# An attention and two-layer expert kernel: the second routing phase spread through the first expert, the first expert's rows ahead of its weights, list columns on VectorE

## Chip, cores and metric

The kernel runs on one core of one Trainium2 chip. The metric is the device time of one execution in microseconds (us), lower is better; runs of a kernel are compared by their median. Engines are named TensorE (PE in the rows, PEld its weight loads), VectorE (DVE), ScalarE (ACT), GpSimd (POOL) and SyncE (SP, which issues DMAs).

## What is computed

Three stages, each fed by the one before. Only the second matters here.

```python
def reference(...):
    attn_out = _attn_ref(q, k, v)             # 4 x 8 heads, 576 positions, 64 wide
    x = attn_out.transpose(0, 2, 1, 3).reshape(2304, 512)
    x = _moe_ref(x, w_gate, w1, w2)           # 8 experts, 1024 wide
    return _moe2_ref(x, w_in, w_out)          # one dense layer, 2048 wide

def _moe_ref(x, w_gate, w1, w2):
    cap = N // E                              # 288 rows for each of 8 experts
    order = np.argsort(-(x @ w_gate).flatten())
    for idx in order:                         # greedy: the highest logit first
        tok, e = idx // E, idx % E
        if assigned[tok] >= 0 or counts[e] >= cap:
            continue
        assigned[tok] = e
        counts[e] += 1
    for e in range(E):
        mask = assigned == e
        out[mask] = np.maximum(x[mask] @ w1[e], 0.0) @ w2[e]
```

## The kernel before

**Stages.** Attention (to about 147 us of the span) writes 2304 rows of 512 numbers to DRAM (`x_dram`) and leaves the gate logits `L` in SBUF. Then come eight routing phases and eight experts E0 to E7 (to about 440 us), then the dense layer in groups A to D, in which TensorE never stops.

**A routing phase** (`Router.phase`, L402) finds which expert fills up next and the list of its 288 rows. It is a chain of small steps: five digit levels, each a VectorE compare (`cmp`, L384), 18 counting matmuls (`cnt`, L467), `fl` on VectorE (L473), one matmul `j8` (L476), `jb` and the next level's `E` on VectorE (L479, L482). A tail follows: `sel`, prefix matmuls `pp` (L512, L513), `ON` (L517) with its matmul `cn` (L546) and reduction `ct` (L548), the columns `R` made on GpSimd by four operations (L536 to L539), a last compare against 96 slots, and 18 matmuls `it` (L551, the list matmul here) that turn one-hot rows into the list. `idx` (L554) is the list as integers, `ii` (L563, through the matmul `ip`) the same list laid out for the output, `exi` (L568) the expert's number. All of `it`, `cnt`, `j8`, `pp`, `cn`, `ip` share one PSUM buffer (tag `rt`). In phase 0 the method `busy` (L387) adds fill matmuls (`idle`) behind the chain's matmuls; `busy(k, 20, im)` puts 20 behind the list matmul.

**Gather and expert.** `gather` (L712) issues three indirect DMAs on GpSimd (`xrow`, 96 rows each) and writes `ilist` from SP. `expert` (L723) reads `exi` into a register on SP, transposes the three row blocks on TensorE (`xtp`, L737), copies them (`xh`, L741), and then for j = 0 to 7 loads a block of 128 hidden units' weights (256 KB of w1, 256 KB of w2), multiplies (`hp`), applies relu (`gh`, `gl`) and, two blocks later, multiplies by w2 into `ya`. E0 and E2 are plain (`MODES`, 'w'): w1 is used as float32 as it was loaded (four `hp` matmuls, shown as eight, x8), and only w2 is split into two parts, a cast on ScalarE (`wbh`, L693) and a subtraction on VectorE (`wbl`, L694). The other six ('s') split w1 too (12 `hp` matmuls). Plain experts load w1 and w2 as two DMAs into buffers of the pools `wa` (4 buffers a tag); the others load one 512 KB block `wraw` into a pool of 8.

**Order.** `ORDER` (L869) lists the steps; a tile scheduler fixes from it one order of instructions per engine, and each engine runs its own in order. A phase is a generator that yields between its steps. 'R0 R1' runs phases 0 and 1 to their end in the program before E0; then each of the 16 steps of an expert advances the routing by one yield (`bg()`), so that phase 2 runs through E0, phase 3 from E0's end through E1, and so on. A phase has 15 yields.

```python
def routing():
    for k in range(8):
        for _ in r.phase(k):
            yield
        rows[k] = f.gather(k, r.out[k][0], r.out[k][2])
        yield
```

Of the kernel before, what the change touches and what calls it, by code (L numbers as in the profile page):

```python
# [336 lines left out]
class Router:  # L337
    def __init__(self, nc, tc, ctx, a):
# [63 lines left out]
    def phase(self, k):  # L402

        nc, wk, sm, L = self.nc, self.wk, self.sm, self.L
        V, Q = nc.vector, nc.gpsimd
# [138 lines left out]
        if not last:  # L544
            cn = self.psr.tile([128, 144], F32, name="cn", tag="rt")
            self.behind(nc.tensor.matmul(cn, self.one, ON.rearrange("p c e -> p (c e)"), start=True, stop=True))  # L546
            ct = sm.tile([128, 8], F32, name="ct")
            V.tensor_reduce(out=ct, in_=cn.rearrange("p (c e) -> p e c", e=8), op=ALU.add, axis=AX.X)  # L548
        it = self.psr.tile([128, 3], F32, name="it", tag="rt")
# [316 lines left out]

ORDER = ('R0 R1 E0/1 E1 E2/2 E3 E4 E5/1 E6/2 E7/2 N A2 A4 A4 A4 A4 B4 B4 B4 B4 B2 C4 C4 C4 C4 C2 D4 D4 D4 D4 D2').split()  # L869
# [131 lines left out]
```

## Time and profile before

| | us |
|---|---|
| timed runs (3): median, lowest, highest | 846.5, 841.11, 850.13 |
| profiled execution | 840.9 |
| its span, first to last instruction | 839.1 |
| TensorE busy in it | 811.0 |
| VectorE busy | 677.6 |
| ScalarE busy | 501.3 |
| GpSimd busy | 181.8 |

The profile is of one execution. Times in rows are microseconds from the span's start, unless ns stands with them. A matmul's end is modelled: successive ones overlap, so the distance from start to start is what one costs. A granted clock of 1.00 is 2.4 GHz, 0.50 is 1.2 GHz.

### The profile page before, as it was taken

How to read it: one execution, taken by the hardware profiler on the slowest of the kernel's cores; microseconds unless marked ns; L12 is line 12 of the kernel's file. 1: busy time of each engine (PE TensorE's matmuls, PEld its weight loads, DVE VectorE, ACT ScalarE, POOL GpSimd, SP SyncE). 2: the span in 40 equal slices, each digit the busy share in tenths (PEclk: the TensorE clock that was granted, in tenths of full speed). 3: DMA queues.
4: the chain of work that ended last, by engine and by line, in shares of the span. 5: the costliest groups of instructions: out<-in, count | busy, mean ns of one | idle time of the engine just before them, and what ended most of it. 6: DMA issues, size and time to landing. Idle time of an engine off the chain costs nothing.

```text
span 839.1 us, 16995 instructions
## 1 busy us (share of the span) xinstructions
PE 811.0 (97%) x6228; PEld 684.5 (82%) x6228; DVE 677.6 (81%) x1813; ACT 501.3 (60%) x1209; POOL 181.8 (22%) x243
## 2 busy tenths in 40 slices
PE   7999999879899999999999999999999999999997
PEld 4787877458898899999998888888878888888886
DVE  6999986848889989998848888788888878657764
ACT  3887876022433535556647677777767777665552
POOL 5565420102211230400000000002223211312223
PEclk9999999979999999999999999999999999999999
DMA  9977622337267796597325444458697674973512
GB/s 223 197 191 223 197 83 103 101 116 254 84 180 237 264 296 214 166 335 247 107 83 177 129 127 131 140 162 201 144 238 179 172 190 107 252 163 123 128 51 76
DMA packets 67411, 142.41 MB, mean 170 GB/s; under 512 B 8224, under 2 KB 20896, under 8 KB 67328
## 3 DMA queue, kind: packets, MB, share of 16 engines
q1 hardware_dynamic: 27008, 70.54, 27.2%
q0 software_dynamic: 29280, 56.63, 26.0%
q10 hardware_dynamic: 11040, 14.16, 4.9%
q8 instruction: 49, 0.80, 0.4%
q14 instruction: 34, 0.28, 0.1%
HBM read 112.98 MB, written 18.88 MB: 157 GB/s over the span
## 4 chain that ended last, share of the span: by engine, by line
PE 77%; DVE 8%; issue 6%; DMA 4%; ACT 2%; POOL 2%; SPq 0%; POOLq 0%; ACTq 0%; DVEq 0%
PE hm L699 7%; PE hm L701 7%; PE hm L700 7%; PE oa L700 6%; PE oa L701 6%; PE oa L699 6%; PE ya L699 4%; PE hp L779 4%; PE ya L700 4%; PE ya L701 4%; PE hp L699 3%; PE hp L701 3%; PE hp L700 3%; PE cnt L467 2%; PE pvl L223 2%
## 5 line engine op out<-in xcount | busy, mean ns | idle before, releaser
L699 PE MATMUL hm<-Yh,wM_sb 128*128 128x512 f32 (+1 forms) x320 | 118.5, 370 | 1.5 <-DMA Yh<-y_dram 1.5
L701 PE MATMUL hm<-Yh,wM_sb 128*128 128x512 f32 (+1 forms) x320 | 118.7, 371 | 0.0
L700 PE MATMUL hm<-Yl,wM_sb 128*128 128x512 f32 (+1 forms) x320 | 118.5, 370 | 0.0
L699 PE MATMUL oa<-wM_sb,gh 128*128 128x512 f32 x288 | 113.1, 393 | 0.0
L700 PE MATMUL oa<-wM_sb,gh 128*128 128x512 f32 x288 | 113.1, 393 | 0.0
L701 PE MATMUL oa<-wM_sb,gl 128*128 128x512 f32 x288 | 112.9, 392 | 0.0
L855 DVE SCALAR_TENSOR_TENSOR eu<-eu 128x512 f32<-128x512 f32 x72 | 49.7, 690 | 45.1 <-ACT eu L854 44.7
L699 PE MATMUL ya<-gh,wbh 128*128 128x288 f32 x256 | 79.5, 315 | 0.3 <-DVE Yl L760 0.3
L700 PE MATMUL ya<-gl,wbh 128*128 128x288 f32 x256 | 77.0, 302 | 0.0
L861 ACT CAST gh<-eu 128x512 fp32r<-128x512 f32 x72 | 44.4, 616 | 53.6 <-DVE eu L858 53.3
L701 PE MATMUL ya<-gh,wbl 128*128 128x288 f32 x256 | 75.9, 298 | 0.0
L699 PEld LDWEIGHTS hm<-Yh,wM_sb 128*128 128x128 f32 x320 | 60.3, 188 | 13.1 <-DMA Yh<-y_dram 2.1
L862 DVE TENSOR_TENSOR gl<-eu,gh 128x512 fp32r<-128x512 f32 x72 | 49.5, 688 | 24.9 <-ACT gh L861 24.3
L700 PEld LDWEIGHTS hm<-Yl,wM_sb 128*128 128x128 f32 x320 | 60.3, 188 | 11.2
L701 PEld LDWEIGHTS hm<-Yh,wM_sb 128*128 128x128 f32 x320 | 60.2, 188 | 10.7
L850 ACT ACTIVATE eu<-hm 128x512 f32<-128x512 f32 x72 | 42.8, 594 | 41.6 <-PE hm L701 41.5
L699 PEld LDWEIGHTS oa<-wM_sb,gh 128*128 128x128 f32 x288 | 54.0, 188 | 12.7 <-ACT osb L826 0.4
L852 ACT ACTIVATE eu<-eu,one_sb 128x512 f32<-128x512 f32 x72 | 52.1, 723 | 20.5 <-DVE eu L851 19.8
L701 PEld LDWEIGHTS oa<-wM_sb,gl 128*128 128x128 f32 x288 | 54.0, 188 | 12.4
L700 PEld LDWEIGHTS oa<-wM_sb,gh 128*128 128x128 f32 x288 | 54.1, 188 | 11.9
L788 ACT ACTIVATE gh<-hp 128x288 fp32r<-128x288 f32 x64 | 26.1, 408 | 61.7 <-PE hp L701 32.1
L827 POOL DMA_DIRECT2D part<-osb x36 | 33.2, 1018 | 135.9 <-ACT osb L826 126.7
(187 smaller groups left out, 2151.5 us busy)
## 6 DMA issues: line engine op xcount, KB each, us to landing
wraw<-in_wE_dram SPq DMA_DIRECT2D x48, 512.0 KB
n<-in_wM_dram SPq DMA_DIRECT2D x32, 512.0 KB
Yh<-y_dram POOLq DMA_DIRECT2D x16, 1024.0 KB, 8.9
Yl<-y_dram POOLq DMA_DIRECT2D x16, 1024.0 KB
part<-osb POOLq DMA_DIRECT2D x36, 256.0 KB, 4.1
vw<-in_vw_dram SPq DMA_DIRECT2D x16, 315.0 KB
kT<-in_kT_dram SPq DMA_DIRECT2D x16, 291.0 KB
qT<-in_qT_dram SPq DMA_DIRECT2D x16, 288.0 KB
```

Of the source, the lines that this page charges most:

```text
L223: self.nc.tensor.matmul(op[c, u], vw[:, 3 * g + u, c], d['aT'][:, u, c], start=True, stop=True)
L699: mm(out, lh, rh, start=first, stop=False)
L700: mm(out, lh, rl, start=False, stop=False)
L701: return mm(out, ll, rh, start=False, stop=last)
L779: self.r.mm = nc.tensor.matmul(hp, w1[:, 128 * dc:128 * dc + 128], xh[:, dc], start=dc == 0, stop=dc == 3)
L788: self.cast = nc.scalar.activation(out=hh[:, 0:288], in_=hp, func=AF.Relu)
L827: nc.gpsimd.dma_start(p, o, accum_op=ALU.add)
L850: nc.scalar.activation(out=e, in_=hp[:, 0:w], func=AF.Exp)
L852: nc.scalar.activation(out=u, in_=e, func=AF.Square, bias=one)
L855: nc.vector.scalar_tensor_tensor(out=u, in0=u, scalar=1.0, in1=r, op0=ALU.add, op1=ALU.mult)
L861: self.cast = nc.scalar.copy(gh[:, 0:w], e)
L862: self.mark = nc.vector.tensor_tensor(out=gl[:, 0:w], in0=e, in1=gh[:, 0:w].bitcast(F32), op=ALU.subtract)
```

## The change

Three things move, and small ones with them.

*Order.* 'R0 R1' becomes 'R0 H4': phase 0 to its end, then four yields of phase 1; the rest of phase 1 advances with the steps of E0, phase 2 follows from E0's end through E1, and phase 7 ends in E5.

*Rows and weights.* All experts load 512 KB blocks `wraw` from the pool of 8; plain experts use w1 in place. In E0 the loads of j = 2 to 7 depend on the third gather (`g0` is overwritten and ends as the third), and the casts of their w2 on the last copy of the transposed rows. 28 fills instead of 20 stand behind phase 0's list matmul.

*List columns.* `R` gets four columns: 0 index, 1 index x g1, 2 index x g2, 3 zero. Columns 0 and 3 are written once, on GpSimd, into two fixed tiles; one VectorE operation writes the other two. After the list matmul two VectorE operations (add 1152, subtract the next column) and a copy to integers give the list. `ON` moves ahead of the prefix matmuls, its matmul joins their PSUM tile, and `ct` is read before the last compare.

```diff
@@ Router.load
+        for t in self.Rw:
+            nc.gpsimd.memset(t[:, :, 3], 0.0)
+            nc.gpsimd.tensor_copy(t[:, :, 0], self.index)
@@ Router.phase
         V.tensor_tensor_scan(out=run[:, 0:n], data0=self.one[:, 0:n], data1=s2, initial=0.0, op0=ALU.mult, op1=ALU.add)
+        if not last:
+            ON = wk.tile([128, 18, 8], F16, name="ON")
+            V.tensor_tensor(out=ON, in0=OH, in1=bc8(ge[:, 0]), op=ALU.mult)
         yield
...
-        pp = self.psr.tile([128, 36], F32, name="pp", tag="rt")
+        pc = self.psr.tile([128, 180], F32, name="pp", tag="rt")
+        pp, cn = pc[:, 0:36], pc[:, 36:180]
+        if not last:
+            self.behind(nc.tensor.matmul(cn, self.one, ON.rearrange("p c e -> p (c e)"), start=True, stop=True))
...
-        if not last:
-            ON = wk.tile([128, 18, 8], F16, name="ON")
-            V.tensor_tensor(out=ON, in0=OH, in1=bc8(ge[:, 0]), op=ALU.mult)
...
-        R = sm.tile([128, 18, 3], F16, name="R")
-        s12 = sm.tile([128, 18], F32, name="s12")
-        Q.tensor_tensor(out=s12, in0=self.index, in1=g1, op=ALU.mult)
-        Q.tensor_tensor(out=R[:, :, 0], in0=self.index, in1=s12, op=ALU.subtract)
-        Q.tensor_tensor(out=R[:, :, 2], in0=self.index, in1=g2, op=ALU.mult)
-        Q.tensor_tensor(out=R[:, :, 1], in0=s12, in1=R[:, :, 2], op=ALU.subtract)
+        R = self.Rw[k % 2]
+        V.tensor_tensor(out=R[:, :, 1:3], in0=g12, in1=two(self.index), op=ALU.mult)
         oa = self.compare(a16, 96, ALU.is_equal, PARTS[k == 0])
+        if not last:
+            ct = sm.tile([128, 8], F32, name="ct")
+            V.tensor_reduce(out=ct, in_=cn.rearrange("p (c e) -> p e c", e=8), op=ALU.add, axis=AX.X)
         yield
...
-        self.busy(k, 20, im)
-        idx = self.pk.tile([96, 3], I32, name="idx")
-        V.tensor_scalar_add(idx, it[0:96], 1152.0)
-        ig = self.igw[k % 2]
-        V.tensor_scalar_add(ig[:, 0:3], it[0:96], 1152.0)
+        self.busy(k, 28, im)
+        ig = self.igw[k % 2]
+        li = ig[:, 0:3]
+        V.tensor_scalar_add(li, it[0:96, 0:3], 1152.0)
+        V.tensor_tensor(out=li, in0=li, in1=it[0:96, 1:4], op=ALU.subtract)
+        idx = self.pk.tile([96, 3], I32, name="idx")
+        V.tensor_copy(idx, li)
@@ FFN.split
-        self.nc.scalar.copy(wh, src)
+        c = self.nc.scalar.copy(wh, src)
+        if self.late is not None:
+            self.tc.add_manual_dep(c.ins, self.late.ins.name, ..., reason="order")
@@ FFN.gather
+            if k == 0:
+                self.g0 = ld
@@ FFN.expert
+            raw = self.rawe.tile([128, 1024], F32, name="wraw")
+            ld = nc.sync.dma_start(raw, src)
+            self.late = xc if k == 0 and j > 1 else None
+            if k == 0 and j > 1:
+                self.tc.add_manual_dep(ld.ins, self.g0.ins.name, ..., reason="rows first")
             if plain:
-                w1 = self.wa.tile([128, 512], F32, name="w1", tag="wah")
-                nc.sync.dma_start(w1, src[:, 0:512])
...
-                    raw = self.wa.tile([128, 512], F32, name="w2r", tag="wal")
-                    nc.sync.dma_start(raw, src[:, 512:1024])
-                    w2 = self.split(raw, self.wb, "wb")
+                w1 = raw[:, 0:512]
+                w2 = self.split(raw[:, 512:1024], self.wb, "wb")
@@ ORDER and body
-ORDER = ('R0 R1 E0/1 E1 E2/2 ...
+ORDER = ('R0 H4 E0/1 E1 E2/2 ...
+            if st[0] == 'H':
+                for _ in range(int(st[1:])):
+                    bg()
+                continue
```

SP at E0's start, before: the register load of the expert's number, then four pairs of loads (w1 `w`, w2 `w2r`, 512 elements a partition each) without any wait for rows, and `ilist` behind them.

```order
L726 TENSOR_LOAD exi [waits DVE_49]
...
L776 DMA w2r<-in_wE_dram 128x512 [waits DMAHW5_49]
L770 DMA w_3686<-in_wE_dram 128x512 [waits DMAHW6_49]
...
L770 DMA w_3798<-in_wE_dram 128x512
L776 DMA w2r<-in_wE_dram 128x512
L720 DMA ilist<-ii 3x96 [waits DMAHW4_49,DVE_49]
```

The same place now: two loads of 1024 elements a partition, and a third that names DMASW2, the semaphore on which the transposes of the third row block wait too.

```order
L776 DMA wraw<-in_wE_dram 128x1024 [waits DMAHW2_49,DMAHW3_49,DMAHW1_49,DMAHW4_49,DMAHW0_49,DMAHW7_49,Activation_49,Pool_49]
L776 DMA wraw<-in_wE_dram 128x1024 [waits DMAHW5_49]
L776 DMA wraw<-in_wE_dram 128x1024 [waits DMAHW6_49,DMASW2_49]
L727 DMA ilist<-ii 3x96 [waits DVE_49]
L776 DMA wraw<-in_wE_dram 128x1024
```

Six of E0's eight loads have moved behind the third gather, and the list's DMA stands behind the first of them.

VectorE in E0's first blocks, before, from the compare of phase 1's second digit level on (`wbl` is the subtraction that splits a block's w2, `gl` the second part of a block's relu; numbers tell tiles apart):

```order
L384 TENSOR_TENSOR cmp_103<-E_3366,rthr_64 128x2304
L458 SCALAR_TENSOR_TENSOR G_3369<-E_3366,dg2_3318 128x18
L473 TENSOR_SCALAR fl_3391<-cnt_3371 128x8
L791 SCALAR_TENSOR_TENSOR gl_3627<-hp_3612,gh_3613 128x288
L479 TENSOR_REDUCE jb_3395<-j8_3393 128x1
L482 TENSOR_SCALAR E_3397<-G_3369,jb_3395 128x36
```

The same place now; wraw_3528 and wraw_3588 are the blocks of j = 2 and j = 3, the first two of the loads that depend on the third gather.

```order
L388 TENSOR_TENSOR cmp_105<-E_3374,rthr_64 128x2304
L462 SCALAR_TENSOR_TENSOR G_3377<-E_3374,dg2_3326 128x18
L699 TENSOR_TENSOR wbl_3531<-wraw_3528,wbh_3530 128x512
L477 TENSOR_SCALAR fl_3399<-cnt_3379 128x8
L699 TENSOR_TENSOR wbl_3591<-wraw_3588,wbh_3590 128x512
L794 SCALAR_TENSOR_TENSOR gl_3445<-hp_3432,gh_3433 128x288
L483 TENSOR_REDUCE jb_3449<-j8_3447 128x1
L486 TENSOR_SCALAR E_3451<-G_3377,jb_3449 128x36
```

Two subtractions have moved between the routing's operations, one ahead of `fl`, one ahead of `jb`; before, the four of the first four blocks stood ahead of this compare.

TensorE in E1 before, from the end of phase 2's list matmul to phase 3's first count:

```order
L551 MATMUL it_4017<-R_3994,cmp_103 128x3
L700 MATMUL hp_4383<-xl_4137,wah_4387 128x288
L701 MATMUL hp_4383<-xh_4136,wal_4388 128x288
...
L561 MATMUL ip_4056<-ident_sb_105,rig0_69 72x96
L701 MATMUL hp_4383<-xh_4136,wal_4388 128x288
L467 MATMUL cnt_4188<-rOH_68,cmp_103 128x8
```

The same place now, with rows of the 12 `hp`, 12 `ya`, 2 `hp` and 9 `ya` matmuls between the two left out:

```order
L552 MATMUL it_4254<-rR0_71,cmp_105 128x4
...
L564 MATMUL ip_4289<-ident_sb_107,rig0_69 72x96
...
L706 MATMUL ya3_4137<-gh_4169,wbl_4177 128x288
L704 MATMUL hp_4411<-xh_3912,wah_4415 128x288
...
L706 MATMUL ya2_4136<-gh_4228,wbl_4236 128x288
L471 MATMUL cnt_4389<-rOH_68,cmp_105 128x8
```

Where five `hp` matmuls and `ip` stood between the list matmul and the count, 35 matmuls and `ip` stand now.

## Rows read from the trace of the kernel before

**Rows 1.** The page, part 1: busy time, share of span, instructions.

```profile
PE 811.0 (97%) x6228; PEld 684.5 (82%) x6228; DVE 677.6 (81%) x1813; ACT 501.3 (60%) x1209; POOL 181.8 (22%) x243
```

**Rows 2.** Stretches: length, then each engine's busy time (instructions), PEclk, DMA share, GB/s.

```profile
core 0: us, PE busy (x) PEld busy (x) DVE busy (x) ACT busy (x) POOL busy (x), PEclk, DMA share, GB/s
...
172.00:176.00 4.00, 2.25 (x28) 1.96 (x29) 0.17 (x1) 1.00 (x2) 0.00 (x0) 0.60 0.15 39
...
180.00:184.00 4.00, 4.00 (x30) 2.83 (x29) 0.70 (x3) 0.41 (x1) 0.00 (x0) 0.62 0.07 9
...
220.00:224.00 4.00, 4.00 (x42) 3.73 (x41) 3.70 (x28) 2.87 (x8) 0.87 (x4) 1.00 0.27 96
224.00:228.00 4.00, 1.87 (x39) 1.66 (x36) 3.59 (x18) 0.93 (x2) 2.62 (x3) 0.93 0.32 101
228.00:232.00 4.00, 4.00 (x23) 3.85 (x22) 3.66 (x10) 0.00 (x0) 1.75 (x2) 0.64 0.65 167
...
348.00:376.00 28.00, 27.57 (x219) 26.69 (x218) 27.07 (x61) 15.97 (x34) 4.43 (x8) 1.00 0.85 287
```

**Rows 3.** TensorE's waits, 150 to 445 us: waiter, releaser, us, times, longest.

```profile
PE it L551 <- DVE ct L548: 1.0, 1, 1.0
PE it L551 <- POOL R L539: 0.6, 1, 0.6
```

**Rows 4.** Timeline of E0's head: start, us, engine, line, instruction, idle before and releaser.

```profile
161.75 0.35 SPq L770 DMA_DIRECT2D w<-in_wE_dram  x1
...
164.85 1.11 POOL L717 DMA_INDIRECT xrow<-x_dram,idx  x1 [2.34 <-DMA w2r<-in_wE_dram]
...
165.39 0.62 ACT L693 CAST wbh<-w2r 128x512 fp32r<-128x512 f32 x1 [18.22 <-DMA w2r<-in_wE_dram]
...
167.63 0.91 POOL L717 DMA_INDIRECT xrow<-x_dram,idx  x1 [0.31 <-issue]
...
173.75 0.90 PE L737 MATMUL xtp<-ident_sb,xrow 96*128 96x96 f32 x4 [4.88 <-DMA xrow<-x_dram,idx]
...
178.40 4.21 PE L779 MATMUL hp<-xh,w 128*128 128x288 f32 x8 [0.57 <-ACT xh L741]
```

**Rows 5.** Timeline of TensorE in E1, at the start of phase 3.

```profile
223.69 0.61 PE L551 MATMUL it<-R,cmp 128*128 128x3 f16 x18
...
227.39 0.63 PE L467 MATMUL cnt<-rOH,cmp 128*128 128x8 f16 x18 [2.13 <-DVE rOH L439]
```

**Rows 6.** Phase 1's list matmul, gathers, E1's transposes; landing of all gathers (last row).

```profile
196.93 0.60 PE L551 MATMUL it<-R,cmp 128*128 128x3 f16 x18
...
198.00 0.92 POOL L717 DMA_INDIRECT xrow<-x_dram,idx  x1 [2.08 <-DVE dg L429]
...
201.55 0.91 POOL L717 DMA_INDIRECT xrow<-x_dram,idx  x1 [0.30 <-issue]
...
212.01 1.15 PE L737 MATMUL xtp<-ident_sb,xrow 96*128 96x96 f32 x12
...
DMA to landing us min/median/max: 5.0/5.3/8.2
```

**Rows 7.** Timeline of one digit level of phase 1 in E0.

```profile
182.40 0.66 PE L467 MATMUL cnt<-rOH,cmp 128*128 128x8 f16 x18
...
183.13 0.17 DVE L473 TENSOR_SCALAR fl<-cnt 128x8 f16<-128x8 f32 x1 [3.92 <-PE cnt L461]
...
183.57 0.17 PE L476 MATMUL j<-fl,rsum 128*128 128x8 f16 x1
...
185.13 0.59 PE L467 MATMUL cnt<-rOH,cmp 128*128 128x8 f16 x18
```

**Rows 8.** Chain that ended last: start, us from piece to piece, what.

```profile
203.53 1.94 PE hp L779 x8
...
361.83 0.27 PE hp L701 x2
...
373.39 0.69 DVE wbl L694
```

**Rows 9.** Timeline: the first compare of a phase.

```profile
225.52 1.34 DVE L384 TENSOR_TENSOR cmp<-E,rthr 128x2304 f16<-128x2304 bf16 x1
```

More of the change, by code (lines that the diff above doesn't have):

```diff
@@ L350, in __init__ @@
         self.igw = [c.tile([96, 72], F32, name=f"rig{i}") for i in range(2)]
+        self.Rw = [c.tile([128, 18, 4], F16, name=f"rR{i}") for i in range(2)]
         for t in self.igw:
@@ L404, in phase @@
         nc, wk, sm, L = self.nc, self.wk, self.sm, self.L
-        V, Q = nc.vector, nc.gpsimd
+        V = nc.vector
         bc8 = lambda t: t.unsqueeze(2).to_broadcast([128, t.shape[1], 8])
@@ L525, in phase @@
             ps = pz[:, 0:18]
-        g1 = sm.tile([128, 18], F32, name="g1")
-        g2 = sm.tile([128, 18], F32, name="g2")
+        g12 = sm.tile([128, 18, 2], F32, name="g12")
+        g1, g2 = g12[:, :, 0], g12[:, :, 1]
         V.tensor_scalar(out=g1, in0=ps, scalar1=97.0, scalar2=None, op0=ALU.is_ge)
@@ L543, in phase @@
             yield
[L544 to L549, printed above, removed]
+        it = self.psr.tile([128, 4], F32, name="it", tag="rt")
         for c in range(18):
             im = self.behind(nc.tensor.matmul(it, oa[c], R[:, c], start=(c == 0), stop=(c == 17)))
-        self.busy(k, 20, im)
+        self.busy(k, 28, im)
[3 more added lines that the diff above has]
+        V.tensor_tensor(out=li, in0=li, in1=it[0:96, 1:4], op=ALU.subtract)
         idx = self.pk.tile([96, 3], I32, name="idx")
-        V.tensor_scalar_add(idx, it[0:96], 1152.0)
-        ig = self.igw[k % 2]
-        V.tensor_scalar_add(ig[:, 0:3], it[0:96], 1152.0)
+        V.tensor_copy(idx, li)
         yield
@@ L684, in __init__ @@
         self.xs = P("f_xs", 1, ctx_e)
-        self.mark = self.cast = None
+        self.mark = self.cast = self.late = None
         self.pend = []
@@ L692, in split @@
         wl = pool.tile([128, 512], F32R, name=nm + "l")
-        self.nc.scalar.copy(wh, src)
+        c = self.nc.scalar.copy(wh, src)
+        if self.late is not None:
+            self.tc.add_manual_dep(c.ins, self.late.ins.name, mybir.DependencyInfo(mybir.DependencyClass.NoSync, mybir.DependencyReason.DATA), reason="order")
         self.nc.vector.tensor_tensor(out=wl, in0=src, in1=wh.bitcast(F32), op=ALU.subtract)
@@ L716, in gather @@
             xr = self.xg.tile([96, 512], F32, name="xrow")
-            nc.gpsimd.indirect_dma_start(out=xr, out_offset=None, in_=self.a['x_dram'],
-                                         in_offset=bass.IndirectOffsetOnAxis(ap=idx[:, g:g + 1], axis=0))
+            ld = nc.gpsimd.indirect_dma_start(out=xr, out_offset=None, in_=self.a['x_dram'],
+                                              in_offset=bass.IndirectOffsetOnAxis(ap=idx[:, g:g + 1], axis=0))
+            if k == 0:
+                self.g0 = ld
             rows.append(xr)
@@ L740, in expert @@
             if plain:
-                (nc.vector.tensor_copy if g == 1 else nc.scalar.copy)(xh[:, :, q], t)
+                xc = (nc.vector.tensor_copy if g == 1 else nc.scalar.copy)(xh[:, :, q], t)
             else:
@@ L767, in expert @@
             hl = None
-            if plain:
-                w1 = self.wa.tile([128, 512], F32, name="w1", tag="wah")
-                nc.sync.dma_start(w1, src[:, 0:512])
-                if mode == 'p':
-                    w2 = self.wb.tile([128, 512], F32, name="w2", tag=("wbh", "wbl")[j % 2])
-                    nc.sync.dma_start(w2, src[:, 512:1024])
-                else:
-                    raw = self.wa.tile([128, 512], F32, name="w2r", tag="wal")
-                    nc.sync.dma_start(raw, src[:, 512:1024])
-                    w2 = self.split(raw, self.wb, "wb")
+            raw = self.rawe.tile([128, 1024], F32, name="wraw")
+            ld = nc.sync.dma_start(raw, src)
+            self.late = xc if k == 0 and j > 1 else None
+            if k == 0 and j > 1:
+                self.tc.add_manual_dep(ld.ins, self.g0.ins.name, mybir.DependencyInfo(mybir.DependencyClass.Sync, mybir.DependencyReason.DATA), reason="rows first")
+            if plain:
+                w1 = raw[:, 0:512]
+                w2 = self.split(raw[:, 512:1024], self.wb, "wb")
                 for dc in range(4):
@@ L780, in expert @@
             else:
-                raw = self.rawe.tile([128, 1024], F32, name="wraw")
-                nc.sync.dma_start(raw, src)
                 w1 = self.split(raw[:, 0:512], self.wa, "wa")
@@ L865, in group @@
             yield
-ORDER = ('R0 R1 E0/1 E1 E2/2 E3 E4 E5/1 E6/2 E7/2 N A2 A4 A4 A4 A4 B4 B4 B4 B4 B2 C4 C4 C4 C4 C2 D4 D4 D4 D4 D2').split()
+ORDER = ('R0 H4 E0/1 E1 E2/2 E3 E4 E5/1 E6/2 E7/2 N A2 A4 A4 A4 A4 B4 B4 B4 B4 B2 C4 C4 C4 C4 C2 D4 D4 D4 D4 D2').split()
 MAN = 0
```

## Prediction

> **What bounds the kernel now.** I read the page first: TensorE is busy for 97% of the span of 839.1 us [rows 1]. The profiled execution took 840.9 us, 1.8 more than its span; the three timed runs have a median of 846.5 (841.11 to 850.13), so my sum is made against 840.9 and scaled to the median at the end. A measurement of this kernel can tell about 1%, some 8.4 us, from no change.
>
> So a gain must come from places where TensorE stands still or runs slowly. The table of stretches finds two of size in the routed experts E0 to E7, 168 to 184 and 224 to 232 [rows 2]; the list of TensorE's waits adds 1.0 us for VectorE's `ct` and 0.6 for GpSimd's `R` [rows 3].
>
> The first place is E0's head [rows 4]. GpSimd issues three gathers from 164.85 to 167.63, the fills run out, and the first transpose starts at 173.75, after 4.9 us of waiting and 8.9 after its gather was issued. Then the granted clock is at its lower level, 0.50 (1.2 of 2.4 GHz), from about 172.9 to 183.0: E0's first eight matmuls take 4.21 us, the same eight elsewhere 1.94 [rows 8]. The second place is the start of routing phase 3 in E1: TensorE has run the list matmul and `ip` and waits 2.13 us, up to 227.39, for `rOH` [rows 5]; after it the clock is low again (0.93 and 0.64 in two stretches of 4 us, so 0.56 + 2.88 = 3.4 us at half speed, 1.7 us lost) [rows 2].
>
> **The change part by part.**
>
> *E0's head.* `ct` stood behind the compare, and the list matmul waited 1.0 us for it [rows 3]; now it stands ahead, and the matmul can end some 0.6 us earlier, near 163.8 (the compare itself ends later than `ct` could). But the list takes three dependent VectorE operations instead of one, with operations of the next phase between them, about 0.8 us more. Net: the gathers start near 165.0, the third at 167.8. Their landing is the unknown. The trace shows three: 5.0, 5.3 and 8.2 us [rows 6]; in E0 it was 8.9 at most, beside eight 256 KB weight loads issued one after the other from 161.75 on [rows 4]. Now two loads of 512 KB go out before the rows, half the bytes, and at E0's pace (the first 512 KB usable at 165.39) most of them are in when the gathers start. I take 5.2: the third block lands at 173.0 (ends: 172.8, and 176.7 with 8.9). Twenty-eight fills of 0.23 us reach from 163.8 to 170.3, where the first block lands, so the eight extra ones (1.8 us) hide in that wait.
>
> From 173.0: third transposes 0.35, copy and hand-over 0.6, so j=0's `hp` starts at 173.95 instead of 178.40. Its four quarters (1.94) and a count block (0.55) end at 176.45 at the full clock; before, this point was the end of the count block of 182.40, 182.95 [rows 7]. Without anything else that is 6.5 us.
>
> But the loads of j=2 to 7 now wait on SP for the third row block. And on VectorE the subtraction that splits j=2's weights has moved ahead of `fl` of the second digit level, while TensorE's `j8` behind j=0 needs that `fl`. Issue at 173.2; from issue to ScalarE's cast 512 KB took 3.64 us (161.75 to 165.39) [rows 4], so 176.9; the cast 0.62 [rows 4], the subtraction 0.69 [rows 8], `fl` to `j8` 0.44 [rows 7]: `j8` at 178.65, a new wait of 2.2 us. j=1 (1.94) and a quarter of j=2 (0.49) follow, to 181.1. The next `jb` stands behind j=3's subtraction, one load later (512 KB are 1.8 us at some 290 GB/s), and a `gl`: 180.4. From `j8` to the count were 1.56 us (183.57 to 185.13) [rows 7], 1.33 of it from `jb`: 181.75, another 0.65 of waiting, and that count is over at 182.25. Before, it was over at 185.6, with a quarter (0.5) less done: gain 185.6 - 182.25 + 0.5 = 3.85. A wait of 2.2 us is as long as the one in E1, after which the low clock cost 1.7; I count half, 0.85. Term: 3.0, between 6.5 (no new wait) and -1.5 (block at 176.7, so 0.15, less 1.7).
>
> A rule of the Trainium skill bears on this (DMA: Bandwidth & Descriptors, Issuing engines are not separate DMA queues): DMAs of all engines run on the same 16 DMA engines and interleave. By it the rows gain from the weights' absence, as 8.9 beside eight weight loads and 5.0 elsewhere suggest. Another rule of that page (Rules for kernel authors, Overlap DMA with compute) speaks against the change: issue early, wait late. By that rule the 2.2 and 0.65 us are the price of holding loads back; no row here shows held loads.
>
> *Start of a phase in E1.* Phase 3 now starts near E1's end, and between the list matmul and the next count TensorE has 12 `hp`, 12 `ya`, 2 `hp` and 9 `ya` matmuls, 35 x 0.135 us = 4.7 [rows 8], with list matmul and `ip` 5.4. VectorE needed 3.7 from there to the count (223.69 to 227.39) [rows 5]; now with a `gl` and two more list operations about 4.5. The wait goes: 2.13 + 1.7 = 3.85 gained; VectorE is next late, by a margin of 0.9. The other starts have as much between. Ends: 0 (the wait turns up in another expert) and 3.85.
>
> *List columns.* The 0.6 us that list matmuls waited for GpSimd go (ends 0 and 0.6). VectorE gets one operation for GpSimd's four, some 0.1 us a phase, beside a TensorE that is the bound; `ON`, the joined PSUM tile, two small copies on GpSimd in the attention part and the plain experts' 512 KB loads hide in the same way, at 0.1 to 0.3 us a phase if that cover goes.
>
> *Later experts.* Half of phase 6 moves from E4 into E5. VectorE is busy 27.1 of 28 us there (348 to 376). The tail of a phase with its list costs it about 3.7 us (220 to 224, 28 operations) [rows 2], two levels with compares of 0.75 some 1.5 more: 32.3 in all. TensorE's share, two counts, list, `pp` and `ip`, is 2.3: 30.3. Up to 2.0 would be lost, unless split weights in buffers and E7's slack take it up. I take -0.7 (ends -2.0 and 0).
>
> *Rows one expert ahead.* For E1, 15.1 us lay between the list matmul (196.93) and the transposes (212.01). Now TensorE has from phase 1's list matmul to E1's first transposes 11 `hp` quarters (5.3 us), 36 `ya` (4.8), two count blocks (1.1) and 0.7 of small ones: 11.9, and 12.7 to the third block's; counted alike 12.0 in E2 and 13.1 or more later. To have the third block takes 2.7 to 2.9 from list matmul to first gather (1.07 before; in E1 a compare of 1.34 [rows 9] now stands before the integer copy), 2.7 to 3.55 from first to third gather (198.00 to 201.55), and 5.0 to 8.2 to land [rows 6]: 10.4 to 14.7. I take -0.5 (ends 0 and, below, -9.25).
>
> Sum: 3.0 + 3.85 + 0.6 - 0.7 - 0.5 = 6.25 us. 840.9 - 6.25 = 834.65, 0.74% less; from the median 846.5 that is **840.2 us**.
>
> **Rivals.**
>
> *No new wait in E0.* The held loads land in time, or don't hold up `fl`. For: the fills keep the clock, and the loads have the DMA engines alone. Against: 3.64 us for 512 KB is what the trace shows. 6.5 + 3.85 + 0.6 - 1.2 = 9.75: 831.2, 1.2% faster.
>
> *The gather is slow by itself.* Its 8.9 us aren't the weights' doing; rows land as late as before and the held loads later still. For: few landings are shown, and one is 8.2. Against: 5.0 and 5.3. -1.5 + 3.85 + 0.6 - 1.2 = 1.75: 839.2, no difference that can be measured.
>
> *Rows late at each expert: slower.* Place: the first transposes of E1 to E3. With 8.9 to land, E1 needs 2.9 + 3.55 + 8.9 = 15.35 against 12.7: 2.65 late; E2, with nothing before its copy, 14.15 against 12.0: 2.15; E3 14.15 against 13.1: 1.05. The first two pull the clock down, 1.7 each: 9.25 lost. It decides from a landing of about 6.5 us on. 3.0 + 3.85 + 0.6 - 0.7 - 9.25 = -2.5: 843.4, slower. Against: two landings of three were short.
>
> **How the numbers follow.** Forecast 0.53, no new wait 0.25, slow gather 0.15, late rows 0.07. Faster by over 1%: most of the second case and the near edge of the first, 0.27. Slower by over 1%: the far edge of late rows with low clock at more experts, 0.05. The rest, 0.68, lies within 1%. The range goes from the second case, scaled 836.7, less the 5.4 by which a run can lie under the median, 831, to late rows, scaled 849.
>
> **What would show it.** Right: E0's third transposes near 173, full clock from 170 to 176; then a wait of about 2 us on TensorE for `fl`, with SP idle until the rows land and VectorE waiting for a cast; no wait for `rOH` in E1; none for GpSimd before list matmuls. Wrong: transposes of E0 later than 175, none of the 2 us, a wait for rows in E1 or E2 over 1 us, or VectorE over 97% in E5 and E6 with TensorE waiting for it.

## Result and profile after

The changed kernel takes 849.92 us (median of 16 runs, 845.2 to 853.92) beside 842.34 us for the kernel before on the same chip (16 runs). By the means it takes 1.0079 times as long, 95% interval 1.0057 to 1.0102. That is 7.6 us slower by the medians and 6.6 by the means, where the prediction had 6.3 faster. The profiled execution took 845.38 us, the second shortest of the 16; its span is 843.6 us, 4.5 more than that of before. TensorE is busy 1.1 us longer than before [rows 1], so again most of the difference lies in standing still, and in the clock:

```profile
PE 812.1 (96%) x6236; PEld 685.1 (81%) x6236; DVE 680.3 (81%) x1829; ACT 501.3 (59%) x1209; POOL 175.2 (21%) x215
```

The table of stretches, with the columns of [rows 2]. The first two rows are E0's head, the next three the end of E3 and the start of E4, the last two lie in E5:

```profile
172.00:176.00 4.00, 3.32 (x38) 2.33 (x36) 2.49 (x6) 0.96 (x2) 0.00 (x0) 1.00 0.44 122
180.00:184.00 4.00, 2.65 (x29) 1.89 (x28) 2.86 (x8) 1.86 (x4) 0.00 (x0) 1.00 0.99 388
308.00:312.00 4.00, 0.00 (x0) 0.00 (x0) 1.09 (x4) 0.48 (x1) 0.00 (x0) 0.82 0.92 227
312.00:316.00 4.00, 3.07 (x17) 2.97 (x18) 1.62 (x4) 1.44 (x3) 0.00 (x0) 0.50 0.02 9
316.00:320.00 4.00, 4.00 (x42) 3.93 (x42) 1.78 (x6) 1.02 (x2) 0.00 (x0) 0.82 0.01 4
...
356.00:360.00 4.00, 2.03 (x8) 1.70 (x8) 4.00 (x12) 0.42 (x1) 0.00 (x0) 0.80 0.80 263
360.00:364.00 4.00, 4.00 (x25) 4.00 (x25) 3.41 (x16) 0.62 (x1) 0.00 (x0) 0.78 0.46 163
```

E0's head runs at the full clock now, where [rows 2] had 0.60 and 0.62. But TensorE does nothing at all for four microseconds at 308, and a new hole is at 356, with VectorE busy for all of the 4.00 us. The list of TensorE's waits from 150 to 445 us gives the names (waiter, releaser, us in total, times, longest):

```profile
PE xtp L744 <- DMA xrow<-x_dram,idx: 6.0, 3, 4.9
PE cnt L471 <- DVE cmp L388: 3.2, 8, 1.3
PE j L480 <- DVE fl L477: 1.8, 2, 1.4
PE hp L704 <- DVE gl L794: 1.4, 1, 1.4
...
PE pp L523 <- DVE run L511: 0.6, 1, 0.6
PE pp L522 <- DVE sel L508: 0.3, 1, 0.3
```

The waits for `ct`, `R` and `rOH` of [rows 3] and [rows 5] are gone. The wait for rows has moved: from E0, where [rows 4] had it, to E4 (4.95 us) and E2 (1.0). E0's head answers to [rows 4] and [rows 7]; this is its timeline on TensorE, VectorE, GpSimd and SP:

```profile
166.48 2.88 POOL L722 DMA_INDIRECT xrow<-x_dram,idx  x1 [42.99 <-DVE wm L437]
...
170.88 0.92 POOL L722 DMA_INDIRECT xrow<-x_dram,idx  x1 [0.31 <-issue]
...
171.63 0.55 PE L744 MATMUL xtp<-ident_sb,xrow 96*128 96x96 f32 x4
...
173.91 0.55 PE L744 MATMUL xtp<-ident_sb,xrow 96*128 96x96 f32 x4
...
174.80 1.39 SPq L776 DMA_DIRECT2D wraw<-in_wE_dram  x3
...
175.03 1.72 PE L784 MATMUL hp<-xh,wraw 128*128 128x288 f32 x6 [0.57 <-ACT xh L748]
...
178.40 0.69 DVE L699 TENSOR_TENSOR wbl<-wraw,wbh 128x512 fp32r<-128x512 f32 x1 [2.63 <-ACT wbh L696]
179.00 0.16 DVE L477 TENSOR_SCALAR fl<-cnt 128x8 f16<-128x8 f32 x1
179.22 0.17 PE L480 MATMUL j<-fl,rsum 128*128 128x8 f16 x1 [1.41 <-DVE fl L477]
...
183.33 0.60 PE L471 MATMUL cnt<-rOH,cmp 128*128 128x8 f16 x18 [1.35 <-DVE cmp L388]
```

The first block lands 5.15 us after its gather (171.63 - 166.48; 8.9 before), and the split of the held block j=2 ends right ahead of `fl`, for which TensorE has stood 1.41 us.

E4's head, on GpSimd and TensorE:

```profile
290.87 0.80 POOL L806 DMA_DIRECT2D Yh<-y_dram  x1 [21.45 <-DMA y_dram<-Yl]
...
292.44 0.78 POOL L806 DMA_DIRECT2D Yl<-y_dram  x1 [0.77 <-DVE na L582]
...
296.05 1.28 POOL L722 DMA_INDIRECT xrow<-x_dram,idx  x1 [2.82 <-PE ip L564]
...
312.93 2.26 PE L744 MATMUL xtp<-ident_sb,xrow 96*128 96x96 f32 x12 [4.95 <-DMA xrow<-x_dram,idx]
```

`Yh` and `Yl` (1 MB each) are the dense layer's input for its second group, issued by GpSimd ahead of time. E4's gathers, issued 3.6 us behind `Yl`, take 16.88 us until the transposes start. The packets of the two DMA queues in use (packets, MB, share of 16 engines; q0 carries what GpSimd issues, q1 the weights that SP issues) in 290.8 to 306.5, and then in 306.5 to 313:

```profile
q1 hardware_dynamic: 936, 3.42, 60.8%
q0 software_dynamic: 1028, 2.10, 42.0%
...
q1 hardware_dynamic: 222, 0.77, 46.4%
q0 software_dynamic: 215, 0.58, 36.4%
```

2.10 MB is `Yh` and `Yl`; 0.58 MB is the rows (3 x 96 x 2 KB = 0.59). So the rows passed after the 2 MB, with E4's weights taking the larger share beside them. Packet by packet the trace has the same order: `Yh` and `Yl` go in 1024 packets of 2 KB, the rows in 144 of 4 KB, and the first of the 144 starts at 305.1, 9.0 us after its gather was issued, when 902 of the 1024 have started.

In the trace of before E4's gathers went out ahead of `Yh` and `Yl`, and 34 us ahead of its transposes:

```profile
281.42 0.92 POOL L717 DMA_INDIRECT xrow<-x_dram,idx  x1 [1.24 <-DVE sg L427]
...
299.76 0.77 POOL L803 DMA_DIRECT2D Yl<-y_dram  x1 [2.06 <-issue]
...
315.64 0.82 PE L737 MATMUL xtp<-ident_sb,xrow 96*128 96x96 f32 x8
```

A delay of 17 us would have cost nothing there.

### The profile page after: what moved, and what is told of

The parts are those of the page before. It is cut to its first block, busy times and chain, and to the rows that moved or that the text cites. A ratio compares the mean times of both kernels' runs of the same rounds, so it can differ in the third digit from the quotient of the medians.

```text
span 843.6 us, 16899 instructions
## 1 busy us (share of the span) xinstructions
PE 812.1 (96%) x6236; PEld 685.1 (81%) x6236; DVE 680.3 (81%) x1829; ACT 501.3 (59%) x1209; POOL 175.2 (21%) x215
## 3 DMA queue, kind: packets, MB, share of 16 engines
q0 software_dynamic: 29280, 56.63, 25.9%
## 4 chain that ended last, share of the span: by engine, by line
PE 58%; issue 6%; DMA 4%; POOL 2%; DVE 1%; ACT 1%; POOLq 0%; DVEq 0%
PE hm L704 7%; PE hm L706 7%; PE hm L705 7%; PE oa L705 6%; PE oa L706 6%; PE oa L704 6%; PE ya L704 3%; DMA xrow<-x_dram,idx 3%; PE ya L706 3%; PE ya L705 3%; PE hp L704 2%; PE hp L705 2%; PE hp L706 2%; PE hp L784 2%; DMA Yh<-y_dram 1%
## 5 line engine op out<-in xcount | busy, mean ns | idle before, releaser
L696 ACT CAST wbh<-wraw 128x512 fp32r<-128x512 f32 x64 | 39.8, 622 | 69.1 <-PE ya L705 40.4
L722 POOL DMA_INDIRECT xrow<-x_dram,idx x24 | 30.7, 1280 | 185.9 <-PE ip L564 95.4
```

Source lines behind the costliest of these rows:

```text
L696: c = self.nc.scalar.copy(wh, src)
L722: ld = nc.gpsimd.indirect_dma_start(out=xr, out_offset=None, in_=self.a['x_dram'], in_offset=bass.IndirectOffsetOnAxis(ap=idx[:, g:g + 1], ...
```

## Experiments

Ratios are to the kernel before, run on the same chip in the same batch, with 95% intervals; they are not quotients of medians. Waits are of one profiled execution each.

### The parts alone

Two runs take one part alone into the kernel before, one takes both, one takes the spread without the list part. The diff of each is the change itself, so much of it.

```diff
 e5_list_only:    Router.load, Router.phase as changed, 20 fills
 e6_rows_only:    FFN.split, FFN.gather, FFN.expert as changed, 28 fills
 e2_order_r1:     both; ORDER = 'R0 R1 E0/1 ...'
 e11_rows_spread: e6_rows_only with ORDER = 'R0 H4 E0/1 ...'
```

> The kernel before with the list columns alone (R on VectorE in fixed tiles, the add, subtract and copy behind the list matmul, ON and its matmul earlier, ct ahead of the last compare); order, loads and 20 fills as before. Theory (this part only takes away the waits for ct, 1.0 us, and for R, 0.6 us): both waits gone, no new one over 0.5 us in E0 to E3, ratio 0.997 to 0.999. Rival (the waits of 1.2 to 1.4 us for fl at the start of phases in E1, E2 and E3, which the changed kernel with the old order has, come from this part): those waits appear here, some 4 us, ratio 1.002 to 1.005.

> The kernel before with the rows and loads alone (512 KB loads for plain experts too, E0's loads of j = 2 to 7 behind the third gather, 28 fills); order and list columns as before. Theory (E0's head gains about 4.5 us in the landing of the rows and the low clock behind it, and gives 1 to 3 back in waits behind the held loads): transposes of E0 end by 175 less whatever the attention part took longer, no low clock there, ratio 0.996 to 0.999. Rival (this part brings the waits in E1 to E3 that the changed kernel with the old order has): ratio 1.002 to 1.005.

> The changed kernel with the order of before: phase 1 to its end ahead of E0 in the program, each phase two experts ahead. Theory (the time was lost by rows one expert ahead, and by VectorE's load in E5): no wait for rows at E2 and E4, none for gl in E5; the wait for rOH at the start of phase 3 in E1 (2.1 us) comes back; E0's head keeps its early rows. Ratio 0.993 to 0.997. Rival (the spread is what gains, and the loss is in the rest of the change): ratio 1.008 or more, the waits in E4 and E5 stay.

> The changed kernel without its list columns: rows and loads as in e6_rows_only, and the new order (second phase spread, each phase one expert ahead). Theory (the spread costs, in late rows, whatever the list columns do): ratio 1.001 to 1.004, with a wait for rows of over 1 us in at least one of E1 to E4. Rival (without the list columns the spread gains, by the start of phase 3 in E1 that no longer waits for rOH): ratio 0.993 to 0.996.

| run | rows first | list part | spread | ratio |
|---|---|---|---|---|
| e6_rows_only | yes | | | 0.9971 (0.9943 to 1.0000) |
| e5_list_only | | yes | | 1.0049 (1.0022 to 1.0076) |
| e2_order_r1 | yes | yes | | 1.0045 (1.0012 to 1.0077) |
| e11_rows_spread | yes | | yes | 1.0070 (1.0027 to 1.0113) |
| the change | yes | yes | yes | 1.0079 (1.0057 to 1.0102) |

Rows first gains 0.3%, as its theory said, with an interval that ends at 1.0000. The spread costs 1.0% beside e6 (with the list part there already, 0.3%, e2 to the change, within their intervals). The 1.0% is a rough size: ten of e11's twelve executions took 843.0 to 858.05 us, the other two 1031.22 and 1559.73. e11 has the same hole as the changed kernel: E4's transposes wait 4.09 us. The list part costs where it was to gain; e5 fits its rival in size, though not in place: its profile has no wait for `fl` in E1 to E3, but 1.2 us for `gl` and 0.5 for `Yl` in E5 (0.2 and 0.3 before) and 0.5 for `wal` in E3, and the mean granted clock of its timed executions is 0.985, that of before in the same batch 0.9885. e2 met neither of its two theories. Its profile has waits of 1.4, 1.2 and 1.4 us for `fl` in E1 to E3, in each of which VectorE stands too and the trace names no cause; that stays open.

### E0: the hold

```diff
 e3_no_hold
-            if k == 0 and j > 1:
+            if False:
                 self.tc.add_manual_dep(ld.ins, self.g0.ins.name, ... Sync ...)
-            self.late = xc if k == 0 and j > 1 else None
+            self.late = None
 e7_split_behind (on e4_y_after_piece, below)
+        if self.late is not None:
+            self.tc.add_manual_dep(s.ins, self.r.fls[self.lj].ins.name, ... NoSync ...)
 e8_hold_all (on e4_y_after_piece)
-            if k == 0 and j > 1:
+            if j > 1:
-                self.tc.add_manual_dep(ld.ins, self.g0.ins.name, ... Sync ...)
+                self.tc.add_manual_dep(ld.ins, self.gk[k].ins.name, ... Sync ...)
```

> The changed kernel without the hold: E0's loads of j = 2 to 7 don't depend on the third gather, and their casts not on the copies of the rows. Theory (the hold is what brings E0's rows early): the gathers land 8 us or more after issue, E0's transposes end at 176 or later with the low clock behind them, while TensorE's waits for fl (1.4 us) and for the compare (1.35 us) go; net 1 to 3 us slower than the changed kernel, ratio 1.009 to 1.012. Rival (the rows come early without it, the hold only costs): transposes of the third block by 174 as in the changed kernel, both waits gone, ratio 1.003 to 1.005.

Ratio 1.0139 (1.0090 to 1.0187): slower than the change, as its theory said (1.009 to 1.012 lies in the interval). The timeline of its first transposes, whose gather was issued at 172.35:

```profile
182.04 0.90 PE L744 MATMUL xtp<-ident_sb,xrow 96*128 96x96 f32 x4 [4.68 <-DMA xrow<-x_dram,idx]
```

9.7 us instead of 5.15, and its table of stretches has a mean clock of 0.52 from 180 to 190. The weights beside the rows are what makes them late; the hold is worth its price in E0.

> As e4_y_after_piece, and on VectorE in E0 the subtraction that splits block j (j over 1) is ordered behind fl of digit level j - 1, so that no routing step ahead of that level waits for a held load. Theory (TensorE's waits for fl and the compare in E0 come from VectorE's order behind the held loads): the waits of 0.6 and 1.35 us in E0 go to under 0.4 us each, 1.5 to 2.5 us less than e4_y_after_piece, ratio about 0.994. Rival (the held loads are late by themselves): TensorE waits for wraw, or for jb, in the same place for as long, ratio within 0.001 of e4_y_after_piece.

Ratio 0.9973 (0.9944 to 1.0003), e4's 0.9966: the rival. TensorE's waits:

```profile
PE cnt L472 <- DVE cmp L388: 3.7, 5, 2.9
...
PE j L483 <- DVE fl L478: 0.4, 1, 0.4
```

The wait for `fl` is gone and comes back one step later, as 2.9 us for the compare, since the same held split now stands ahead of `jb`.

> As e4_y_after_piece, and in every expert, not E0 alone, the loads of j = 2 to 7 wait for that expert's third gather. Theory (one expert ahead, the next expert's loads start at the same time as its gathers, because both follow from the same phase, and slow the rows): the rows of E1 and E2 land in 5 to 6 us, TensorE's waits for them (2.0 and 0.9 us in the profile of e4_y_after_piece) and the low clock behind them go, 3 to 5 us less, ratio 0.991 to 0.994. Rival (the rows are late because the list itself is late, or held loads come too late to feed an expert): waits for rows stay over 1 us, or waits for wraw or its split over 1 us appear behind the first two blocks of an expert, ratio 0.997 or more.

Ratio 1.0161 (1.0127 to 1.0196): the rival, in its second form. TensorE no longer waits for a row, but held loads come too late to feed an expert. Ahead of the 5.6 us for `fl`, in E3, ScalarE waits 5.8 us for `wraw`:

```profile
PE j L480 <- DVE fl L477: 6.8, 2, 5.6
PE hp L705 <- DVE xl L753: 3.1, 1, 3.1
...
PE hp L707 <- DVE wal L700: 1.9, 1, 1.9
```

The prediction set a rule of the Trainium skill against the change (DMA: Bandwidth & Descriptors, Rules for kernel authors: issue a DMA early and wait for it late). It is borne out here, with 1.0161 beside e4's 0.9966, and not in E0, where 1.0139 without the hold stands beside 1.0079 with it.

### The distance from list to expert

```diff
 e1_y_after_rows, in FFN.group
-            nc.gpsimd.dma_start(t, self.a['y_dram'][:, v, :, 128 * t0:128 * t0 + n])
+            yd = nc.gpsimd.dma_start(t, self.a['y_dram'][:, v, :, 128 * t0:128 * t0 + n])
+            if t0 == 2 and not part:
+                self.tc.add_manual_dep(yd.ins, self.g4.ins.name, ... NoSync ...)
 e12_spread_fixed: e11_rows_spread with that, and ORDER = 'R0 H4 ... E5 E6/2 E7/3 ...'
 e15_fixed_h8:     e12_spread_fixed with ORDER = 'R0 H8 ...'
 e17_change_h8:    the changed kernel with ORDER = 'R0 H8 ...', nothing else
```

> The changed kernel, with the loads of Yh and Yl for the second dense group (2 MB on GpSimd's queue) ordered behind E4's third gather instead of 3.6 us ahead of its first. Theory (rows queue behind the 2 MB on the same queue, and one expert ahead leaves no time for it): E4's rows land within about 9 us, TensorE's wait of 4.95 us in front of E4's transposes is gone or under 1 us, and the low clock behind it too, some 7 us in all, so about 0.8% less than the changed kernel: ratio to before about 1.000. Rival (the burst of E4's eight 512 KB weight loads, which start only when phase 4 has its expert's number, slows the rows): the wait stays at 3 us or more, ratio 1.005 or more.

Ratio 1.0011 (0.9979 to 1.0043), the theory's 1.000. E4's wait is gone; in this execution rows were 1.3 us late for E1 and 1.6 for E2, with a low clock behind both.

> As e11_rows_spread, with the loads of Yh and Yl behind E4's gathers and E5's piece done in E7, that is e4_y_after_piece without the list columns. Theory (the list columns cost 4 to 6 us in each of the two orders): ratio 0.990 to 0.993. Rival (in this order they cost nothing): ratio 0.996 to 0.998, as e4_y_after_piece.

Ratio 0.9893 (0.9846 to 0.9941), faster than both kernels and at the edge of what the theory gave. Left over are rows that are late for E1 and E2:

```profile
PE xtp L743 <- DMA xrow<-x_dram,idx: 2.9, 2, 2.4
...
PE j L476 <- DVE fl L473: 0.8, 1, 0.8
```

> As e12_spread_fixed, with eight yields of phase 1 ahead of E0 instead of four, so that every list and every gather comes a quarter of an expert (about 8 us) earlier. Theory (what is left of the spread's cost is rows that land too late for E1 and E2): no wait for rows over 0.3 us in E1 to E4 and no low clock there, 3 to 5 us less, ratio 0.984 to 0.987. Rival (E0's head pays for the eight yields with as much, or waits for rOH at the starts of phases come back): ratio 0.989 to 0.993.

Ratio 0.9879 (0.9845 to 0.9913), 834.73 us against 843.25: the best kernel of the study, though its interval covers e12's. No wait for rows, no low clock behind phase 0:

```profile
PE cnt L467 <- DVE cmp L384: 2.5, 4, 1.2
...
PE j L476 <- DVE fl L473: 0.4, 1, 0.4
```

> The changed kernel with one number altered: eight yields of phase 1 ahead of E0 instead of four. The loads of Yh and Yl of the second dense group then stand behind E4's gathers by themselves, and E5 keeps its piece. Theory (the distance from list to expert is most of what the change lost): no wait for rows of over 1 us, E4's 4.95 us gone; with the waits for gl in E5 left, ratio 0.990 to 0.995. Rival (the loss is in the list part and VectorE): ratio 1.000 to 1.005.

Ratio 0.9933 (0.9897 to 0.9969), as the theory had it. One number of the change takes it from 1.0079 to under 1: E4's first gather is then issued at 294.54, `Yh` behind it at 299.70, and E4's transposes start at 311.60 without a wait. Against its theory, E2's rows were 1.3 us late. It is the same mechanism one pair of loads earlier: `Yh` and `Yl` of the first dense group (512 KB each) now stand right ahead of E2's gathers, whose landing the last row gives:

```profile
225.72 0.78 POOL L806 DMA_DIRECT2D Yl<-y_dram  x1 [0.58 <-DVE rnrem L587]
227.23 0.99 POOL L722 DMA_INDIRECT xrow<-x_dram,idx  x1 [0.74 <-PE ip L564]
...
DMA to landing us min/median/max: 14.9/16.0/16.0
```

In the changed kernel `Yl` of that group had landed before E2's gathers went out, and they took 7.8 to 8.6 us.

### VectorE in E5

```diff
 e4_y_after_piece (on e1_y_after_rows); e10_rows_piece (on e6_rows_only)
-ORDER = ('... E5/1 E6/2 E7/2 N ...
+ORDER = ('... E5 E6/2 E7/3 N ...
```

> As e1_y_after_rows, and the piece of the dense layer's weights that is split by VectorE in E5 is done in E7 instead. Theory (in E5 VectorE has phase 6 and that piece at once, and gl comes late): the waits for gl, run and sel at 356 to 358 (2.2 us) and the low clock behind them (1.7 us) are gone, so 3 to 4 us less than e1_y_after_rows, ratio about 0.996. Rival (the phase alone fills VectorE, or E7 has no room for the piece): a wait of over 1 us for VectorE stays in E5 or comes up in E7, and the ratio is within 0.001 of that of e1_y_after_rows.

> As e6_rows_only, and the piece of the dense layer's weights that VectorE splits in E5 is done in E7. Theory (the waits for gl and Yl at 358 to 359, 1.2 us in the profile of e6_rows_only, come from VectorE having that piece and the routing at once): both waits gone, no new one over 0.5 us in E7, 1 to 2.5 us less, ratio 0.994 to 0.996. Rival (E7 has no room for it): ratio 0.997 or more.

e4: 0.9966 (0.9933 to 0.9999) after e1's 1.0011, the 4 us of the theory, though the two intervals overlap; the waits for `gl`, `run` and `sel` are gone, and none came up in E7. e10: 0.9964 (0.9928 to 0.9999), not told apart from e6's 0.9971, though its waits for `gl` and `Yl` are gone too.

### The list part

```diff
 e9_list_late (on e5_list_only): the index column is cast behind the attention part
-            nc.gpsimd.tensor_copy(t[:, :, 0], self.index)
+                    i = V.tensor_copy(t[:, :, 0], self.index)
 e13_fixed_count:   e12_spread_fixed + ON, cn, ct as changed
 e14_fixed_columns: e12_spread_fixed + R, add, subtract, copy as changed
 e16_h8_all:        e15_fixed_h8 + both
 e18_list_first (on e4_y_after_piece), for the next phase's first compare
+                    self.tc.add_manual_dep(self.cmpi.ins, self.li.ins.name, ... NoSync ...)
```

> As e5_list_only, with the two casts that write the index column on VectorE behind the attention part, instead of on GpSimd within it, where GpSimd stood still for them until rsmall had landed (1.2 us in the profile of e5_list_only). Theory (the list columns cost what e5_list_only lost because of that stand in the attention part): ratio 0.998 to 1.001. Rival (they cost in the routed part, by VectorE's load): ratio 1.003 to 1.006, as e5_list_only.

> As e12_spread_fixed, with one half of the list part put back: ON ahead of the prefix matmuls, its matmul in their PSUM tile, ct ahead of the last compare; R stays on GpSimd. Theory (the cost of the list part, 0.5 to 0.7% in three pairs of runs, lies in the columns on VectorE and not in this half): TensorE's wait for ct in E0 (1.0 us) goes, ratio 0.987 to 0.990. Rival (it lies in this half, which puts ON and ct on VectorE ahead of the last compare in every phase): ratio 0.993 to 0.997, as e4_y_after_piece.

> As e12_spread_fixed, with the other half of the list part put back: R written on VectorE into fixed tiles, the list by an add, a subtraction and a copy on VectorE; ON, its matmul and ct stay where they were before. Theory (the cost lies here: two more dependent VectorE operations between the list matmul and the gathers, and the rows are later by that): ratio 0.993 to 0.997, with waits for rows in E1 and E2 longer than in e12_spread_fixed (2.4 and 0.6 us). Rival (it lies in the other half): ratio 0.988 to 0.991.

> As e4_y_after_piece, that is with the whole list part, but with eight yields ahead of E0; it is e15_fixed_h8 with the list part. Theory (the list part costs because it makes the list, and so the rows, later, which no longer matters when lists come 8 us earlier): ratio 0.986 to 0.990, no wait for rows over 0.3 us. Rival (it costs by VectorE's load, wherever the lists stand): ratio 0.993 to 0.997, with waits for VectorE in the place of those for rows.

> As e4_y_after_piece, with the integer copy of the list ordered ahead of the next phase's first compare on VectorE, so that the list part delays the gathers by its dependent operations alone. Theory (the list part costs by a later list, most of it the compare of 1.35 us that stands between the subtraction and the copy): from list matmul to first gather 1.3 to 1.7 us instead of 2.0 to 2.9, ratio 0.990 to 0.994, between e12_spread_fixed and e4_y_after_piece. Rival (VectorE's load): the distance shrinks and the ratio stays at 0.995 to 0.998, with the waits for rows in E1 and E2 as long as in e4_y_after_piece (2.0 and 0.9 us).

| run | beside | ratio |
|---|---|---|
| e9_list_late | e5 1.0049 | 1.0065 (1.0033 to 1.0096) |
| e13_fixed_count | e12 0.9893 | 0.9944 (0.9915 to 0.9973) |
| e14_fixed_columns | e12 0.9893 | 1.0007 (0.9977 to 1.0036) |
| e16_h8_all | e15 0.9879 | 0.9921 (0.9889 to 0.9953) |
| e18_list_first | e4 0.9966 | 0.9928 (0.9898 to 0.9957) |

The attention part isn't the cause (e9). The columns on VectorE cost 1.1% in e14. Its waits for rows are 2.8 us in E2 (0.6 in e12) and 1.9 in E1 (2.4 in e12), with a low clock behind both. The longest wait is another, in E0, and it too has a low clock behind it (0.57 from 184 to 188); in e12 it was 0.75 us:

```profile
183.44 0.17 PE L480 MATMUL j<-fl,rsum 128*128 128x8 f16 x1 [3.28 <-DVE fl L477]
```

It is the wait behind a held load's split, and it was 0.3 to 2.0 us in the other kernels with held loads, so that a single execution doesn't tell how much of it belongs to the columns.

How the list gets later shows in the timeline of phase 1's end in E0, VectorE, TensorE and GpSimd, first in the changed kernel:

```profile
196.31 0.60 PE L552 MATMUL it<-rR,cmp 128*128 128x4 f16 x18
...
196.95 0.16 DVE L556 TENSOR_SCALAR rig<-it 96x3 f32<-96x3 f32 x1
...
197.32 0.14 DVE L557 TENSOR_TENSOR rig<-rig,it 96x3 f32<-96x3 f32 x1
...
197.53 1.35 DVE L388 TENSOR_TENSOR cmp<-E,rthr 128x2304 f16<-128x2304 bf16 x1
...
198.80 0.16 DVE L559 CAST idx<-rig 96x3 int32<-96x3 f32 x1
...
199.23 0.91 POOL L722 DMA_INDIRECT xrow<-x_dram,idx  x1 [27.43 <-DVE idx L559]
```

and in e12, with the columns on GpSimd:

```profile
197.40 0.60 PE L551 MATMUL it<-R,cmp 128*128 128x3 f16 x18
...
198.06 0.14 DVE L554 TENSOR_SCALAR idx<-it 96x3 int32<-96x3 f32 x1
...
198.27 1.34 DVE L384 TENSOR_TENSOR cmp<-E,rthr 128x2304 f16<-128x2304 bf16 x1
198.47 1.94 POOL L719 DMA_INDIRECT xrow<-x_dram,idx  x1 [2.62 <-DVE rig L556]
```

From list matmul to first gather it is 1.07 us here and 2.0 to 2.9 in all eight phases of the changed kernel. But rows wait for the third gather, and that one goes out 7.1 us after this list matmul in e12 and 7.3 in the changed kernel, because e12's second issue takes 3.51 us. A later third gather shows in E2: 3.7 us after the list matmul in e12, 5.6 in the changed kernel, 6.8 in e14.

e13 cost 0.5% with the distance to the first gather at 1.07, its rival's ratio, though within the intervals of both kernels; its profile has one wait of 2.0 us for `fl` in E0 in place of e12's 0.8. e16 lies between its theories: with the lists some 5 us earlier (first gather to transposes in E4: 18.5 us in e15, 13.1 in e12) the part still costs 0.4%, less than the two intervals together. e18 shortened the distance in E1 alone (1.73); in the other phases it stayed at 2.0 to 2.7, so that it doesn't tell. The halves don't add up either: 0.5% and 1.1% one by one, 0.73% together (e12 to e4), over three batches. So a later list is seen to cost time in E2 of e14; that it is the whole price is not shown, and VectorE's load stays a rival. What the part costs in the old order, where rows have an expert to spare (e5, e9), is not settled. The waits for `gl` and `Yl` point to VectorE, but e5's profiled execution doesn't hold the loss: from phase 0's first count to the dense layer it takes 283.7 us, 2.3 less than the kernel before.

## Why the prediction was wrong

Times here run from phase 0's first counting matmul (146.52 us before, 148.03 after), since the attention part ahead of it took 1.5 us longer in this execution; see below.

*E0's head: right in mechanism and sum, in part by luck.* Third block forecast at 26.5 us, found at 25.9: its gather went out 1.6 us later than forecast and landed in 3.0 us instead of the 5.2 taken (the first landed in 5.15). The two waits behind held loads were 2.2 and 0.65 in the forecast and 1.41 and 1.35 in the trace; only their sums agree, 2.85 and 2.76. The count that the step follows was over at 35.8 (39.1 before), with two `hp` matmuls, a quarter, more done: 3.3 + 0.5 = 3.8 us gained, 3.0 taken. The 0.85 for a low clock behind the waits was not lost.

*Start of a phase in E1: right.* The wait for `rOH` is gone and the clock is 1.00 there: 3.85 us as forecast.

*Later experts: the place right, the size past its end.* "I take -0.7 (ends -2.0 and 0)". In E5 TensorE waits 0.3, 0.6 and 1.4 us for `sel`, `run` and `gl`, and the low clock from 358 to 362 takes another 1.6: 3.9. The sum of busy times had been right (VectorE 4.00 of 4 us at 356), the low clock behind a wait was left out of its end. e4 shows that it is VectorE's load: without the piece the waits go.

*Rows one expert ahead: the step that failed.* "I take -0.5 (ends 0 and, below, -9.25)". Measured: 1.0 us in E2 and 4.95 in E4, and behind that a low clock that takes 1.5 us from 312 to 316 and 0.7 from 316 to 320: 8.2. The time from list matmul to gather was forecast well (2.7 to 2.9; 2.9 in E1, 2.0 to 2.7 in the others), the time that TensorE would leave also. What failed is the landing, 5.0 to 8.2 us in the sum. I took it from a kernel whose gathers had their queue to themselves, and worked out the experts one by one without asking what GpSimd issues ahead of a gather. The longest of [rows 6] was 8.2 us; it is 16.8 in E4, because 2 MB for the dense layer lie in front (e1: with the 2 MB behind the gathers the wait is gone). Both loads were in the trace of before: GpSimd issued `Yh` and `Yl` at 296.89 and 299.76 there, 12 us ahead of the next gather. The Trainium skill states the mechanism (DMA: Bandwidth & Descriptors, SWDGE vs HWDGE vs iDMA): one queue carries all DMAs that GpSimd issues, and a DMA engine goes round-robin between it and the others. The trace agrees with 2.10 MB ahead of the rows and 42.0% of the engines for that queue beside 60.8% for the weights. Of the rivals "rows late at each expert" was the one that came nearest: right in sign and in what waits, wrong in place (E1 to E3; found 1.0 us in E2 and the rest in E4) and without the cause of E4's landing. Its point of decision, a landing of about 6.5 us, was reached in E1 (third gather 6.6, no wait) and passed in E2 (8.0, late by 1.0).

*List columns: wrong.* "The 0.6 us that list matmuls waited for GpSimd go" is right, and 0.1 to 0.3 us a phase was to hide beside TensorE. It doesn't hide: five pairs of kernels that differ in the whole part put its price at 0.74% (e2 against e6), 0.73% (e4, e12), 0.49% (e5), 0.42% (e16, e15) and 0.09% (the change, e11), none of them a gain, though the last two lie within the intervals. I had priced the later list in E0 and in E1 and had not carried it into the other gathers' chances to be late; whether that is the whole of it is not shown (e13, e14).

The sum by measured terms: 3.8 + 3.85 + 0.6 - 3.9 - 8.2 = -3.85, beside -3.0 by the traces (from that first count to the dense layer's first matmul 286.05 us before, 289.03 after). The 1.5 us of the attention part make the 4.5 of the span. The means lost 6.6, and a single execution doesn't say where the rest went; rows late for E1 and E2 in the executions of e1 and e4, and only for E2 here, show that the lateness varies from one to the next.

The range (831.0 to 849.0) missed by 0.9 us, and with a median for before of 842.34 instead of 846.5 it would have missed by more. It went to the price of late rows alone; late rows and VectorE's overload came together, and both follow from work that was moved later.

## What to carry to other kernels

When a producer is moved closer to its consumer, what was slack becomes a deadline. List what stands ahead of the moved DMA on its own queue, in bytes, and what is let loose at the same moment (here the expert's own weights, whose loads wait for the same phase). A landing time read where the queue was empty is no bound for one that is full. And look for the dose: here four yields lost 0.8% and eight gained 0.7%, with the same code, and eight put another pair of loads ahead of another expert's rows.
